# Attention with a filler: a step of two key blocks and four heads in place of four key blocks and two heads

## The chip, the cores and the metric

The kernel runs on one core of a Trainium2 chip. A core has engines with queues of their own: TensorE (PE in the profile; its weight loads are PEld), VectorE (DVE), ScalarE (ACT), GpSimd (POOL) and SyncE (SP), which here issues most of the transfers. The metric is device microseconds of one execution. The times before the change are 1333.11, 1337.48 and 1337.88 us; the median is 1337.48 us.

## The reference

The input x has 2048 tokens of 640 features. Two branches start from the same layer norm, and are added to x:

```python
xn = layernorm(x)
q, k, v = split(xn @ wqkv)              # 32 heads of 20 features
p = softmax(q @ k.T * 20 ** -0.5)       # 2048 x 2048 for each head
A = concat_heads(p @ v) @ wo
y = layernorm(xn)
B = gelu(y @ w1 + b1) @ w2 + b2         # 640 -> 1536 -> 640
out = x + A + B
```

## The kernel before, in words

**Precision.** All products are made of 16-bit or 32-bit parts so that the sum is nearly fp32. Queries and keys are stored as a high and a low fp16 half; a stack of three times 20 rows (high with high, high with low, low with high) and one row for a shift gives 61 rows, so that two heads lie in rows 0 to 60 and 64 to 124 of one tile. The exponentials `p` are fp32. Key blocks (128 keys each, 16 in all) are of two kinds, by `SPLIT = (1, 1, 0, 0) * 4`. In a split block V lies as two fp16 halves, and p is used as its upper 16 bits (read in place as bf16) and a lower half `low`, an fp16 tile that VectorE makes with one subtraction (`rest`, line 762). In an unsplit block p and V are multiplied as fp32, and each such product shows as two rows of the profile.

**Stages.** A first stage (to about 225 us) normalizes x, projects queries, keys and values, and splits the weights. Then the attention runs, and between its instructions the MLP (branch B) and, at the end, the output projection are laid as a filler. What is left of the projection follows the last attention step.

**The attention before.** The loops run over pairs of heads and halves of the queries (`ORDER`, 32 visits), over two chunks of 512 queries (`cc`), and over groups of `GRP = 4` key blocks. For each key block `scores` issues two matmuls (two heads, at the same time in two row halves of TensorE) into a tile of two PSUM banks (pool `psS`, three tiles), and one exponential of 128 x 1024 on ScalarE (line 750). `pv` multiplies a finished group with V (line 779). Its result tile `o` has 128 rows in four quarters of 32; each quarter takes products of its own, and four products for four quarters run at the same time in four column strips of TensorE. Before, the quarters 2a and 2a+1 hold two partial sums of head a, which are added much later. After 16 key blocks ScalarE copies `o` to `ev` (line 800), and `unload` writes the parts and the sums of the exponentials to `opart` and `lpart` in DRAM. For every 4 to 6 heads, `finish` reads them back, adds the two parts, divides by the sums, splits the result into fp16 halves and writes it to `oscr`, from where the projection takes it.

**What sets the order.** The program is written under a manual schedule: each engine executes in the order in which Python emits. A step emits: scores of two key blocks; `tick()`, which advances the side work (the gelu of the MLP on VectorE and ScalarE, the finishes, the loads of the next stack, each a generator that does one piece a tick; `patient` generators wait where other side work took time); the lower half of the first block; `other()`, which emits a chunk of the filler by a running credit (`rate = 1.265`); scores of the other two key blocks; `tick()`; the lower halves still open; and `pv` of the group before. The gelu of a pair of hidden blocks (lines 966 to 981) starts when its last filler matmul has been emitted, and takes five ticks: it reads the PSUM tile `pu` (966), adds the bias and squares (968, 970), forms the tanh's argument (972), waits for the tanh on ScalarE (977), and then makes and splits the result (979 to 981). SP issues the loads of the next stack (`load_stack`, line 143), the stores of `ev` and the transfers of the finishes in one queue.

Of the kernel before, what the change touches and what calls it, by code (L numbers as in the profile page):

```python
# [33 lines left out]
GRP = 4  # L34
# [3 lines left out]
TAIL = 12  # L38
ORDER = ([(g, hf) for g in range(TAIL) for hf in range(2)] + [(g, hf) for hf in range(2) for g in range(TAIL, NPAIR)])
MC = 256  # L40
QKTOP = 512.0
EXPMASK = 0x7F800000


def mha_mlp_kernel(tc, x, wqkv, wo, w1, b1, w2, b2, out):
# [4 lines left out]
    with (  # L50
# [13 lines left out]
        opart = dram.tile([2, D, S], F32, name="opart")  # L64
        lpart = dram.tile([2, 2, H, S // 2], F32, name="lpart")
        linv = dram.tile([2, H, S // 2], F32, name="linv")
# [15 lines left out]
        ones = keep.tile([P, P], F32, name="ones")  # L82
# [60 lines left out]
        stacks = {}  # L143

        def load_stack(g, hf, ks=None):

            new = ks is None
            qs = stp.tile([P, S // 2], F16, tag="qs", name=f"qs{g}")
            if new:
                ks = stp.tile([P, S], F16, tag="ks", name=f"ks{g}")  # L150
            stacks[g, hf] = (qs, ks)
            cols = slice(hf * 1024, (hf + 1) * 1024)
            for a in range(2):
                b, r = 64 * a, (2 * g + a) * DH
                for i in range(3):
                    rows = slice(b + i * DH, b + (i + 1) * DH)
                    nc.sync.dma_start(qs[rows, :], qkscr[(0, 0, 1)[i], r : r + DH, cols])
                    if new:
                        nc.sync.dma_start(ks[rows, :], qkscr[(0, 1, 0)[i], D + r : D + r + DH, :])
                    yield  # L160
            for a in range(2):
                b = 64 * a
                nc.sync.dma_start(qs[b + 60 : b + 61, :], bscr[2 * g + a : 2 * g + a + 1, cols])
                if new:
                    nc.sync.dma_start(ks[b + 60 : b + 61, :], bscr[H : H + 1, :])
                yield

# [7 lines left out]
        with tc.tile_pool(name="pa", bufs=2) as pa, tc.tile_pool(name="pa1", bufs=1) as pa1, tc.manual_schedule():  # L175
            wv = pa1.tile([P, KD, 3, 2, D], F16, name="wv")

# [168 lines left out]
            def qk_out(c, tt, ps):  # L346
                hl = stp.tile([P, 2, 2, 512], F16, tag="ks", name="qkhl")
# [15 lines left out]
            def qk_sq(c, tt, hl):  # L363
                if tt % 2:
                    sq = stp.tile([P, S // 2], F16, tag="qs", name="sq").bitcast(BF16).rearrange("p (i t) -> p i t", i=2)
                else:
                    sq = pa.tile([P, 2, 512], BF16, tag="sq", name="sq", bufs=2)
                if c == 0:
                    nc.scalar.activation(sq, hl[:, 0], AF.Square)
                else:  # L370
                    nc.vector.tensor_mul(sq, hl[:, 0], hl[:, 0])
                pend.extend((c, 2 * tt + i, sq[:, i]) for i in range(2))
# [212 lines left out]
            for c in range(4):  # L585
# [48 lines left out]
                if c == 3:  # L634
                    stack = load_stack(0, 0)
# [32 lines left out]
        with ExitStack() as scope:  # L668
# [3 lines left out]
            ptp = pool(name="pt", bufs=2 * GRP - 1)  # L672
# [64 lines left out]
            nfin = 2 * len(UNITS)  # L737
# [4 lines left out]
            def scores(g, hf, cc, kb):  # L742

                qs, ks = stacks[g, hf]
                pt = ptp.tile([P, 2, 512], F32, tag="p", name="p")
                ps = psS.tile([P, 2, 512], F32, tag="s", name="s")
                for a in range(2):
                    nc.tensor.matmul(ps[:, a, :], ks[64 * a : 64 * a + 61, kb * P : (kb + 1) * P],  # L748
                                     qs[64 * a : 64 * a + 61, cc * 512 : (cc + 1) * 512], start=True, stop=True)
                nc.scalar.activation(pt, ps, AF.Exp, scale=QS)  # L750
                return pt
# [5 lines left out]
            def rest(unit):  # L757

                kb, pt = unit[3:]
                if SPLIT[kb]:  # L760
                    low = ptp.tile([P, 2, 512], F16, tag="low", name="low", bufs=GRP)
# [3 lines left out]
            evs = {}  # L765

            def pv(units):

                g, hf, cc, kb0 = units[0][:4]
                if kb0 == 0:
                    pv.o = psO.tile([P, 512], F32, tag="o", name="o")
                    pv.begun = set()
                last = units[-1][3] == NKB - 1

                def product(q, src, v0, t):
                    nc.tensor.matmul(pv.o[32 * q : 32 * q + 32, :], src[:, v0 - PAD * (1 - q % 2) :][:, :32], t,  # L779
                                     start=q not in pv.begun, stop=last, skip_group_check=True)  # L780
                    pv.begun.add(q)

                split = [(u[3], upper(u[4]), u[5]) for u in units if SPLIT[u[3]]]
                whole = [(u[3], u[4]) for u in units if not SPLIT[u[3]]]
                of16 = lambda kb, a: 2 * PAD + kb * 2 * VROW + (2 * g + a) * 2 * VW
                of32 = lambda kb, a: PAD + kb * VROW + (2 * g + a) * VW
                for kb, up, _ in split:
                    for a in range(2):
                        product(2 * a, vhalf, of16(kb, a), up[:, a])
                        product(2 * a + 1, vhalf, of16(kb, a) + VW, up[:, a])  # L790
                for a in range(2):
                    for n, (kb, _, low) in enumerate(split):
                        product(2 * a + n % 2, vhalf, of16(kb, a), low[:, a])
                for a in range(2):
                    for n, (kb, pt) in enumerate(whole):
                        product(2 * a + n % 2, vfull, of32(kb, a), pt[:, a])
                if last:
                    if cc == 0:
                        evs[g, hf] = m1.tile([P, 2, 512], F32, tag="ev", name="ev")
                    nc.scalar.activation(evs[g, hf][:, cc], pv.o, AF.Copy)  # L800
                    if cc == 1:
                        unload(g, hf, evs.pop((g, hf)))

            def dma(g, hf):

                return (nc.scalar if (g, hf) == ORDER[-1] else nc.sync).dma_start

            def unload(g, hf, ev):
                cols = slice(hf * 1024, (hf + 1) * 1024)
                direct.extend([ev] if (g, hf) == ORDER[-1] else [])  # L810
                for p in range(0 if direct else 2):
                    dma(g, hf)(lpart[p, hf, 2 * g : 2 * g + 2, :].rearrange("a (c t) -> a c t", c=2),
                                      ev[PAD + DH + VW * p :: 64])
                    for a in range(2):
                        q0, r = 64 * a + PAD + VW * p, (2 * g + a) * DH
                        dma(g, hf)(opart[p, r : r + DH, cols].rearrange("d (c t) -> d c t", c=2),
                                          ev[q0 : q0 + DH])
                if g + 1 in ENDS:
                    fins.append(finish(g + 1 - UNITS[ENDS.index(g + 1)], g + 1, hf))
                    if len(fins) == 1:  # L820
                        patient.append(finishing())
                        runner[:] = patient[-1:]
# [520 lines left out]
```

## Time and profile before

| | before |
|---|---|
| median of three runs | 1337.48 us |
| span of the profiled execution | 1337.9 us |
| PE busy | 1325.8 us (99%) |
| ACT busy | 1128.0 us (84%) |
| DVE busy | 1055.1 us (79%) |
| exponentials (L750) | 1024 of 1050 ns |
| lower halves (L762) | 512 of 1218 ns |
| evacuations (L800) | 64 of 618 ns |
| DMA moved | 129.54 MB |

The span of the profiled execution agrees with the largest of the three runs, 1337.88 us. A group of instructions reads: line, engine, operation, out<-in, shapes, count | busy time, mean ns of one | idle time of the engine before them, and what ended it. In the timeline, each row has its start, its length, and how many instructions were merged. A matmul's length holds its latency, so throughput is read from the distance of starts. In the table by windows, the columns are the window, its length, and the busy time with the count of instructions of PE, PEld, DVE, ACT and POOL, then the granted clock of TensorE, the share of the DMA engines, and GB/s.

### The profile page before, as it was taken

The page shows a single profiled execution, that of the slowest core. Times are in us where ns is not written, and L with a number is a line of the kernel's source. Part 1 is how long each engine was busy: PE and PEld are TensorE (multiplying, and loading weights), DVE is VectorE, ACT ScalarE, POOL GpSimd, SP SyncE. Part 2 cuts the span into 40 slices and gives each one's busy share as a digit, 9 for nine tenths or more (in the row PEclk, how much of TensorE's full clock was granted, in tenths as well). Part 3 has the DMA queues.
Part 4 walks back from the last instruction along what each step waited for, and adds up shares of the span by engine and source line. Part 5 has one row for each costly group of instructions (what it writes and reads, how often), then busy time and mean ns, then how long its engine had stood idle before and what let it go on. Part 6 is the DMA issues. An engine that isn't in the chain of part 4 may idle for free.

```text
span 1337.9 us, 29042 instructions
## 1 busy us (share of the span) xinstructions
PE 1325.8 (99%) x11635; PEld 586.7 (44%) x11635; DVE 1055.1 (79%) x1431; ACT 1128.0 (84%) x1306; POOL 37.5 (3%) x86
## 2 busy tenths in 40 slices
PE   9999899999999999999999999999999999999998
PEld 6645456444434343434343443344443434333366
DVE  7656754998788989878897879888879888997742
ACT  7844334999999999999999999999999999999900
POOL 3010000000000000000000000000000000000000
PEclk9999899999999999999999999999999999999999
DMA  9778723021203232212322132223032323334375
GB/s 279 254 196 176 136 79 104 15 59 39 66 28 103 61 83 81 63 48 59 111 63 81 33 93 66 75 69 94 19 80 71 93 66 87 118 95 118 105 218 188
DMA packets 100326, 129.54 MB, mean 97 GB/s; under 512 B 24292, under 2 KB 66664, under 8 KB 100188
## 3 DMA queue, kind: packets, MB, share of 16 engines
q1 hardware_dynamic: 96652, 120.25, 31.6%
q0 software_dynamic: 2912, 6.90, 2.8%
q8 instruction: 92, 1.51, 0.5%
q10 hardware_dynamic: 624, 0.51, 0.1%
q14 instruction: 46, 0.38, 0.1%
HBM read 82.14 MB, written 42.51 MB: 93 GB/s over the span
## 4 chain that ended last, share of the span: by engine, by line
PE 87%; DVE 6%; DMA 4%; ACT 1%; issue 1%; SPq 0%; ACTq 0%; DVEq 0%
PE o L779 30%; PE s L748 20%; PE py L1061 13%; PE pu L1031 11%; PE z L1146 5%; PE qkp L337 5%; PE vp L410 3%; DVE low L762 2%; DMA xt<-in_A_x_dram 1%; DMA xnt<-row 1%; DMA qkscr<-qkhl 1%; DVE st L255 1%; DVE qkhl L353 1%; ACT p L750 1%; DMA wos<-in_A_wo_dram 0%
## 5 line engine op out<-in xcount | busy, mean ns | idle before, releaser
L750 ACT ACTIVATE p<-s 128x1024 f32<-128x1024 f32 x1024 | 973.9, 1050 | 33.1 <-PE s L748 27.1
L762 DVE TENSOR_TENSOR low<-p 128x1024 f16<-128x1024 f32 x512 | 614.3, 1218 | 144.8 <-ACT p L750 144.0
L779 PE MATMUL o<-p,vfull 128*32 128x512 bf16 (+1 forms) x4096 | 429.0, 493 | 0.0
L748 PE MATMUL s<-qs,ks 61*128 61x512 f16 x2048 | 311.4, 381 | 0.2 <-ACT p L750 0.2
L748 PEld LDWEIGHTS <-ks 61*128 61x128 f16 x2048 | 61.2, 94 | 278.4 <-issue 276.1
L1061 PE MATMUL py<-w2t,hT 128*128 128x320 f16 x1152 | 178.5, 300 | 0.0
L1031 PE MATMUL pu<-xm,w1t 128*128 128x256 f16 x1440 | 178.2, 273 | 0.1
L1031 PEld LDWEIGHTS <-w1t 128*128 128x128 f16 x1440 | 131.0, 98 | 64.0 <-issue 50.2
L1061 PEld LDWEIGHTS <-hT 128*128 128x128 f16 x1152 | 102.3, 98 | 88.1 <-issue 53.9
L337 PE MATMUL qkp<-xnt,wv 128*128 128x512 f16 x600 | 131.1, 379 | 1.3 <-issue 1.3
L779 PEld LDWEIGHTS <-vfull 128*32 128x32 f16 x3072 | 59.9, 95 | 138.4 <-issue 106.9
L779 PE MATMUL o<-low,vfull 128*32 128x512 f16 x1024 | 101.3, 377 | 0.1
L337 PEld LDWEIGHTS <-wv 128*128 128x128 f16 x600 | 58.2, 98 | 71.0 <-issue 1.6
L779 PEld LDWEIGHTS o<-p,vfull 128*32 128x32 f32 x2048 | 61.7, 108 | 53.2
L410 PE MATMUL vp<-wv,xnt 128*128 128x320 f16 x480 | 69.5, 306 | 3.7 <-DVE qkhl L353 3.7
L1146 PE MATMUL z<-w1t,ot 128*128 128x320 f16 x480 | 67.4, 299 | 0.0
L352 ACT ACTIVATE qkhl<-qkp,qks 128x1024 f16<-128x1024 f32 (+1 forms) x24 | 23.1, 964 | 46.3 <-PE qkp L337 26.6
L410 PEld LDWEIGHTS <-xnt 128*128 128x128 f16 x480 | 47.9, 100 | 23.8 <-issue 3.7
L1146 PEld LDWEIGHTS <-ot 128*128 128x128 f16 x480 | 46.0, 98 | 22.9 <-issue 5.5
L353 DVE SCALAR_TENSOR_TENSOR qkhl<-qkp,qks,qkhl 128x1024 f16<-128x1024 f32 (+1 forms) x24 | 26.5, 1104 | 32.9 <-ACT qkhl L352 32.9
L1103 DVE SCALAR_TENSOR_TENSOR acc<-z,sc,acc 128x320 f32<-128x320 f32 x32 | 17.5, 549 | 37.3 <-PE z L1146 37.2
L800 ACT ACTIVATE ev<-o 128x512 f32<-128x512 f32 x64 | 39.5, 618 | 2.2 <-PE o L779 2.1
(195 smaller groups left out, 670.4 us busy)
## 6 DMA issues: line engine op xcount, KB each, us to landing
qkscr<-qkhl SPq DMA_DIRECT2D x40, 256.0 KB
opart<-ev SPq DMA_DIRECT2D x124, 80.0 KB
ks<-qkscr SPq DMA_DIRECT2D x120, 80.0 KB
qs<-qkscr SPq DMA_DIRECT2D x192, 40.0 KB
oa<-opart SPq DMA_DIRECT2D x32, 240.0 KB
xt<-in_A_x_dram SPq DMA_DIRECT2D x16, 320.0 KB
xscr<-xnt SPq DMA_DIRECT2D x4, 1280.0 KB
xm<-xscr SPq DMA_DIRECT2D x8, 640.0 KB
```

The lines of the kernel that those rows point to most:

```text
L337: nc.tensor.matmul(ps[:, i, :], wv[:, k, q, a, mm * P : (mm + 1) * P], xnts[c][:, k, b, :], start=(k + n == 0), stop=(k == KD - 1 and n == 2))
L352: nc.scalar.activation(hl[:, 0, i0:i1], ps[:, i0:i1], AF.Copy, scale=a)
L353: nc.vector.scalar_tensor_tensor(hl[:, 1, i0:i1], ps[:, i0:i1], a, hl[:, 0, i0:i1], ALU.mult, ALU.subtract)
L410: nc.tensor.matmul(ps[:, hf, :320], xnts[c][:, k, a, j * P : (j + 1) * P], wv[:, k, 2, b, hf * 320 : (hf + 1) * 320], start=(n == 0), stop ...
L748: nc.tensor.matmul(ps[:, a, :], ks[64 * a : 64 * a + 61, kb * P : (kb + 1) * P], qs[64 * a : 64 * a + 61, cc * 512 : (cc + 1) * 512], star ...
L750: nc.scalar.activation(pt, ps, AF.Exp, scale=QS)
L762: nc.vector.tensor_sub(low, pt, upper(pt))
L779: nc.tensor.matmul(pv.o[32 * q : 32 * q + 32, :], src[:, v0 - PAD * (1 - q % 2) :][:, :32], t, start=q not in pv.begun, stop=last, skip_gr ...
L800: nc.scalar.activation(evs[g, hf][:, cc], pv.o, AF.Copy)
L1031: nc.tensor.matmul(ps[:, i], w1v[:, k, (f + i) // 4, a, fo_ : fo_ + P], xnt[:, k, b, :], start=(n == 0), stop=(n == 3 * KD - 1))
L1061: nc.tensor.matmul(ps[:, :320], hTs[mc][:, f, a, j * P : (j + 1) * P], w2v[:, f, b, hf * 320 : (hf + 1) * 320], start=(n == 0), stop=(n == ...
L1146: nc.tensor.matmul(ps[:, :320], ot[:, k, a, j * P : (j + 1) * P], wov[:, k, b, h * 320 : (h + 1) * 320], start=(n == 0), stop=(n == 3 * KD ...
```

## The change

A step is now `GRP = 2` key blocks for four heads. The visits run over eight sets of four heads (`q`); the first six visits take all four chunks of 512 queries, and the last two sets are visited twice, for two chunks each (`VISITS`). For a key block, `scores` is called for two pairs of heads, and the two exponentials of 128 x 1024 fill the halves of one tile of 128 x 2048. With `SPLIT` as it was, steps alternate: one has two split blocks, the next two unsplit ones. `pv` gives each of the four heads one quarter of `o`, which takes all its products, so no parts are added later, and `o` is copied out once for four heads (32 times). `rest` makes the lower half of four heads with one instruction of 128 x 2048; that of the second block of a step is emitted in the step after it. The pool of p holds four tiles of 2048 for seven of 1024, that of `low` two for four.

Queries and keys are loaded apart: queries for each chunk of 512, keys in two halves of 1024. A half of the keys is emitted in a few ticks after the first step of a visit (second half), or after the fifth step of the last chunk before (first half). The finishes work on 512 queries of one chunk, 24 of them for 12, and have no addition. The tile `ones` moves to a pool of the first stage. The projection of a piece of 256 tokens may start when its chunk of 512 is finished.

```diff
-GRP = 4
+GRP = 2
+VISITS = ([(q, tuple(range(NCC))) for q in range(LATE)]
+          + [(q, ccs) for ccs in ((0, 1), (2, 3)) for q in range(LATE, NQ)])
...
+        def load_keys(v, half):
+            q = VISITS[v][0]
+            ks = stp.tile([P, 2, S // 2], F16, tag="ks", name="ks")
+            kss[v, half] = ks
+            cols = slice(half * 1024, (half + 1) * 1024)
+            for a in range(2):
+                for i in range(3):
+                    nc.sync.dma_start(ks[64 * a + i * DH : 64 * a + (i + 1) * DH], rows_of(qkscr[(0, 1, 0)[i]], D, q, a, cols))
+                    if i != 1:
+                        yield
...
-            ptp = pool(name="pt", bufs=2 * GRP - 1)
+            ptp = pool(name="pt", bufs=2 * GRP)
...
+            def scores(v, cc, kb, pair, pt):
+                qs, ks = qss[v, cc], kss[v, kb // 8]
                 ps = psS.tile([P, 2, 512], F32, tag="s", name="s")
                 for a in range(2):
+                    rows = slice(64 * a, 64 * a + 61)
+                    nc.tensor.matmul(ps[:, a, :], ks[rows, pair, kb % 8 * P : (kb % 8 + 1) * P], qs[rows, pair, :],
+                                     start=True, stop=True)
+                nc.scalar.activation(pt[:, 2 * pair : 2 * pair + 2], ps, AF.Exp, scale=QS)
...
-                    low = ptp.tile([P, 2, 512], F16, tag="low", name="low", bufs=GRP)
+                    low = ptp.tile([P, 4, 512], F16, tag="low", name="low", bufs=2)
                     nc.vector.tensor_sub(low, pt, upper(pt))
...
+                def products(src, at, t):
+                    for h in range(4):
+                        nc.tensor.matmul(pv.o[32 * h : 32 * h + 32, :], src[:, at(h) : at(h) + 32], t[:, h],
+                                         start=not pv.begun, stop=last, skip_group_check=True)
+                    pv.begun = True
+                split = [u for u in units if SPLIT[u[2]]]
+                for u in split:
+                    for s in range(2):
+                        products(vhalf, of16(u[2], s), upper(u[3]))
+                for u in split:
+                    products(vhalf, of16(u[2], 0), u[4])
+                for u in units:
+                    if not SPLIT[u[2]]:
+                        products(vfull, lambda h: PAD + u[2] * VROW + (4 * q + h) * VW, u[3])
...
-                    nc.vector.tensor_add(o0, o0, o1)
...
                     for kb in range(kb0, kb0 + GRP):
-                        units.append([g, hf, cc, kb, scores(g, hf, cc, kb)])
-                        if kb % 2 == 0:
-                            continue
+                        pt = ptp.tile([P, 4, 512], F32, tag="p", name="p")
+                        units.append([v, cc, kb, pt])
+                        for pair in range(2):
+                            scores(v, cc, kb, pair, pt)
                         tick()
-                        if kb % GRP == 1:
-                            rest(units[0])
+                        if kb % GRP == 0:
+                            if prev and SPLIT[prev[1][2]]:
+                                rest(prev[1])
                             credit += rate
                             other()
                         else:
-                            for u in units[1:]:
-                                rest(u)
+                            if SPLIT[kb - 1]:
+                                rest(units[0])
                             if prev:
                                 pv(prev)
```

335 lines of the change are left out of this document (138 added, 197 removed).

## The prediction

> **What bounds the kernel now.** I read the busy times and the chain first, then a stretch of the attention phase, then the groups, then the timelines of one step.
>
> ```profile
> span 1337.9 us, 29042 instructions
> ...
> PE 1325.8 (99%) x11635; PEld 586.7 (44%) x11635; DVE 1055.1 (79%) x1431; ACT 1128.0 (84%) x1306; POOL 37.5 (3%) x86
> ...
> PE 87%; DVE 6%; DMA 4%; ACT 1%; issue 1%; SPq 0%; ACTq 0%; DVEq 0%
> ```
> ```profile
> 300.00:1200.00 900.00, 899.83 (x8439) 360.94 (x8441) 767.06 (x915) 870.87 (x975) 12.73 (x15) 1.00 0.26 72
> ```
> ```profile
> L750 ACT ACTIVATE p<-s 128x1024 f32<-128x1024 f32 x1024 | 973.9, 1050 | 33.1 <-PE s L748 27.1 <-ACT p L750 0.4
> L762 DVE TENSOR_TENSOR low<-p 128x1024 f16<-128x1024 f32 x512 | 614.3, 1218 | 144.8 <-ACT p L750 144.0
> ...
> L800 ACT ACTIVATE ev<-o 128x512 f32<-128x512 f32 x64 | 39.5, 618 | 2.2 <-PE o L779 2.1
> ...
> L966 DVE TENSOR_TENSOR u<-pu,r2f 128x512 f32<-128x512 f32 x48 | 32.8, 683 | 0.2
> L977 ACT ACTIVATE w<-w 128x512 f32<-128x512 f32 x48 | 32.0, 666 | 0.0
> ```
>
> In the 900 us from 300 to 1200 TensorE is busy 899.83 us at a granted clock of 1.00, ScalarE 870.87 and VectorE 767.06; the chain is 87% TensorE, and what ScalarE waits for before an exponential is TensorE's scores (27.1 of 33.1 us). A busy TensorE may hide waits, so I check one step (four exponentials) by start times:
>
> ```profile
> 704.17 0.60 PE L779 MATMUL o<-p,vfull 128*32 128x512 f32 x4
> 704.70 0.60 PE L748 MATMUL s<-qs,ks 61*128 61x512 f16 x4
> 705.24 1.81 PE L1031 MATMUL pu<-xm,w1t 128*128 128x256 f16 x15
> 706.98 0.61 PE L748 MATMUL s<-qs,ks 61*128 61x512 f16 x4
> 707.52 0.64 PE L779 MATMUL o<-p,vfull 128*32 128x512 bf16 x8
> 707.98 0.38 PE L779 MATMUL o<-low,vfull 128*32 128x512 f16 x4
> 708.20 1.03 PE L779 MATMUL o<-p,vfull 128*32 128x512 f32 x8
> 709.16 0.60 PE L748 MATMUL s<-qs,ks 61*128 61x512 f16 x4
> 709.70 1.81 PE L1031 MATMUL pu<-xm,w1t 128*128 128x256 f16 x15
> 711.44 0.39 PE L748 MATMUL s<-qs,ks 61*128 61x512 f16 x2
> ```
>
> Scores take 0.54, the filler 1.74, scores 0.54, then upper halves 0.46, lower halves 0.22 and unsplit blocks 0.96 (together 1.64): 4.46 us with no hole, and the next step repeats it. So TensorE's own work is the limit. A lighter ScalarE or VectorE gains nothing; either can only cost, by being late.
>
> **The change part by part.** *TensorE.* Per two steps the same products remain: 16 upper, 8 lower and 8 unsplit products of 512 columns (an unsplit one is two rows), only that the first 24 stand in one step and the unsplit ones in the next: 2 x 0.46 + 2 x 0.22 = 1.36, and 2 x 0.96 = 1.92; sum 3.28 = 2 x 1.64. Scores and filler keep counts and places. Gain 0. Bound below: the second half of the unsplit rows takes 0.53 (704.17 to 704.70), the first only 0.43 (0.96 - 0.53), so 0.10 us is paid on leaving. If only unsplit rows pay it, the change halves that: 128 x 0.10 = 13 us gained. I take 0, because 16-bit rows of the same 32-column form pay it too: 16 rows of 128 columns last 0.34 to the next start, while four turns at a quarter of 0.23 make 0.23:
>
> ```profile
> 200.92 0.41 PE L382 MATMUL norms<-sq,heads 128*32 128x128 bf16 x16
> 201.26 1.04 PE L337 MATMUL qkp<-xnt,wv 128*128 128x512 f16 x4
> ```
>
> *ScalarE.* The exponentials stay; 32 of 64 evacuations go, 32 x 0.618 = 20 us. *VectorE.* A row of 512 takes 683 ns, of 1024 1218, so 148 ns is fixed and 2048 take 148 + 4 x 535 = 2.29 us: 256 of them 586 us for 614; the finishes lose their additions. All of this lies beside TensorE: 0. [...]
>
> *The lower half comes later, in a larger piece.* This is the term that counts. Before, both lower halves of a group are issued in its own step and read a full step later. In the changed order, a split step issues that of its first key block beside its own second scores, and that of its second block only in the next step, after the first scores, while the products that read it are emitted behind that same step's second scores.
>
> Let t be the start of the second scores of a split step. Two exponentials end 2.4 us after their scores start (706.98 to 707.47 + 1.94; 709.16 to 709.59 + 1.94):
>
> ```profile
> 707.47 1.94 ACT L750 ACTIVATE p<-s 128x1024 f32<-128x1024 f32 x2 [0.20 <-PE s L748]
> 709.59 1.94 ACT L750 ACTIVATE p<-s 128x1024 f32<-128x1024 f32 x2 [0.17 <-PE s L748]
> ```
>
> The first block's scores lie 0.54 + 1.74 earlier, so its lower half can start at t + 0.1 and, at 2.29, end at t + 2.4; the second's can start at t + 2.4 and end at t + 4.7. TensorE asks for the second after 0.54 scores, 1.92 unsplit products of the step before, 0.54, 1.74, 0.54 and then the upper halves 0.92 and the first lower 0.22: t + 6.4. With nothing else on VectorE there is room of 1.7 us, and none is lost. But the activation of the filler stands in the same queue:
>
> ```profile
> 711.79 0.68 DVE L966 TENSOR_TENSOR u<-pu,r2f 128x512 f32<-128x512 f32 x1
> ...
> 713.84 1.22 DVE L762 TENSOR_TENSOR low<-p 128x1024 f16<-128x1024 f32 x1
> 714.98 0.68 DVE L972 SCALAR_TENSOR_TENSOR w<-w,u 128x512 f32<-128x512 f32 x1
> 715.58 1.21 DVE L762 TENSOR_TENSOR low<-p 128x1024 f16<-128x1024 f32 x1
> ...
> 718.45 0.68 DVE L979 SCALAR_TENSOR_TENSOR u<-w,u 128x512 f32<-128x512 f32 x1
> 719.17 0.49 DVE L980 TENSOR_SCALAR hT<-u,sc 128x512 f16<-128x512 f32 x1
> 719.69 0.75 DVE L981 SCALAR_TENSOR_TENSOR hT<-u,sc,hT 128x512 f16<-128x512 f32 x1
> ```
>
> L966 starts 0.35 after the last pu row (711.44 to 711.79), the group to L970 holds a lower half back by 2.05, L972 by 0.60, and the group L979 to L981 lasts 1.99. In the compiled order of the changed kernel 128 pairs of lower halves stand; between the two of a pair there is nothing 61 times, what was L972 24 times (with the group L966 to L970 ahead of the pair), the group L979 to L981 21 times, and one short row otherwise.
>
> Case A, 24 times: the activation begins at t + 0.35, the first lower half starts at t + 2.4, the second 2.2 + 0.6 later (2.2 since back-to-back rows overlap by 0.08: 713.84 + 1.22 against 714.98), it ends at t + 7.5: TensorE stands 1.1 us. Case B, 21 times: the tanh is queued behind the second exponentials, ends at t + 2.4 + 0.67, then 1.99, then 2.2: t + 7.3, 0.9 us. Where the filler chunk is 9 rows and not 15, TensorE asks 1.74 x 6/15 = 0.7 us sooner and both grow by that. Bounds: 24 x 1.1 + 21 x 0.9 = 45, and 24 x 1.8 + 21 x 1.6 = 77 us. I take 50, near the lower end: with a short chunk TensorE's step (0.54 + 1.04 + 0.54 + 1.64 = 3.76) is under four exponentials (973.9/1024 x 4 = 3.80), so there it has waits on ScalarE to give. Below the lower end: if start-up and hand-over are 0.4 us shorter per event than read here, 45 x 0.7 = 32. Behind a late lower half only TensorE waits; scores, filler and exponentials all shift with it, so it adds to the end.
>
> [...]
>
> *Keys and queries.* Keys come in halves, each emitted over the 3 steps before its use, where whole stacks came 8 groups ahead. SP needs, at 0.33 each, 16 loads, 5 stores and 2 loads of a finish in the 3 x 4.46 = 13.4 us:
>
> ```profile
> L159 SPq DMA_DIRECT2D ks<-qkscr x120: 281/329/1500, 211.4 to 1225.0; - x120
> ```
>
> That is 7.6 us, and 5.8 are left for waits of SP and for landing, which the page does not time for this queue. Bounds: 0, and half a step (2.2) at 9 visits, 20 us. I take 2, as the room is most of the need. Behind a late key half, all scores of the visit wait.
>
> *Ends.* The same 16 loads stand before the first scores, and 444 output rows after the last in both orders: 0. The last finish broadcasts over 512 columns and not 1024: half of these rows go,
>
> ```profile
> L931 PE MATMUL rb<-lt,sel 64*80 64x64 f32 x32 | 2.5, 234 | 0.0
> ```
>
> so 1.2 us less. The buffer pools (four tiles of 2048 for seven of 1024) give each tile back by a product that TensorE has issued before the next scores: 0.
>
> **Sum.** 1337.9 + 50 + 2 - 1 = 1389; the profiled span is 0.4 us above the median of 1337.48, which is as much as the runs differ otherwise, so I forecast 1388.
>
> **The rivals.** (1) *The cover holds.* VectorE idles 15% of the stretch (767 of 900), and if the compiled order lets it run ahead, the lower half is never last: 1337.5 - 1 + 2, about 1338. Against it: VectorE cannot start before the exponentials, and the room of 1.7 us is smaller than the 2.65 of case A whatever the mean load.
>
> (2) *The products get cheaper.* The 0.10 us on leaving belongs to the unsplit rows alone, and lateness is below the room: 1337.5 - 13 - 1 = 1323. It decides as soon as 13 us exceed the lateness, that is, below 0.3 us per case. For it: the 0.53 against 0.43. Against it: the 16-bit rows at 200.92, and the lateness has to be absent too.
>
> (3) *The key halves land late as well*: 1388 + 20 - 2, and with case A and B at their upper bound 1388 + 20 + 25 = 1433. For it: short notice. Against it: 5.8 us of room.
>
> **How the numbers follow.** A change of 0.5% (6.7 us) is about what this measurement can tell from none. Forecast (slower by lateness, own range 1365 to 1415): 0.74. Rival 1: 0.12, nearly all within 0.5%. Rival 2: 0.08, faster. Rival 3: 0.06, slower. So faster 0.08, same 0.11, slower 0.81. Forecast and rival 1 hold 0.86; the range from 1336 to 1414 takes in both but their edges.
>
> **What would show it.** Right: TensorE's rows that read `low` last longer than 0.38 in some 45 places, near the activation's rows, by about a microsecond; the chain names VectorE's lower halves and the activation for several per cent; `low` rows last 2.2 to 2.3 us x256, evacuations x32; the pair of unsplit and split product groups takes 3.28 together; ScalarE's idle time before exponentials grows, to TensorE. Wrong: those rows all near 0.38 (rival 1); product groups that sum to 3.18 (rival 2); TensorE's weight loads of scores waiting for a DMA of `ks` (rival 3).

## The result and the profile after

The changed kernel takes 1398.49 us (median of four runs, 1396.35 to 1401.37) against 1335.42 for the kernel before in the runs beside it (1333.11 to 1337.88): a ratio of 1.0479, 95% interval 1.0456 to 1.0502. It is 4.8% slower. The forecast was 1388, with 1336 to 1414 as its range. Of the edited kernels below, one execution (with nine blocks split) ran at a granted clock of 0.654 and took 1857.06 us; it is left out.

First the page of the changed kernel, its busy times and its chain of waits, and then the 900 us of the attention phase by engine (busy time and count of TensorE, its weight loads, VectorE, ScalarE and GpSimd, then granted clock, share of the DMA engines, GB/s):

```profile
span 1397.3 us, 28234 instructions
...
PE 1335.1 (96%) x11619; PEld 595.0 (43%) x11619; DVE 1036.5 (74%) x1191; ACT 1124.8 (80%) x1274; POOL 36.8 (3%) x85
...
PE 60%; DVE 23%; ACT 6%; DMA 5%; issue 4%; SPq 1%; DVEq 0%; ACTq 0%; POOLq 0%
PE o L800 17%; DVE low L785 12%; PE s L772 12%; PE py L1016 8%; PE pu L986 8%; PE qkp L361 7%; ACT p L774 5%; PE z L1101 5%; PE vp L434 3%; DVE u L922 1%; DVE u L924 1%; DVE w L926 1%; DVE w L928 1%; DMA xnt<-row 1%; DVE u L935 1%
```
```profile
300.00:1200.00 900.00, 854.90 (x7929) 346.38 (x7928) 706.90 (x655) 815.44 (x892) 11.89 (x14) 1.00 0.21 56
```

TensorE, which before was busy 899.83 of these 900 us, now stands 45 of them, at the same granted clock of 1.00. The chain was 87% TensorE and 6% VectorE; now it is 60% and 23%, with the lower halves (L785) at 12% and the activation of the filler (L922 to L928 and L935) behind them. VectorE did not become the fuller engine: it is busy 707 us of the stretch, less than the 767 before. It is late, not full.

The groups by form (count, busy time, mean ns of one, idle time of the engine before them and its cause):

```profile
L774 ACT ACTIVATE p<-s 128x1024 f32<-128x1024 f32 x1024 | 974.2, 1032 | 100.4 <-PE s L772 97.1
L785 DVE TENSOR_TENSOR low<-p 128x2048 f16<-128x2048 f32 x256 | 580.5, 2286 | 125.1 <-ACT p L774 124.5
...
L800 PE MATMUL o<-low,vfull 128*32 128x512 f16 x1024 | 87.1, 379 | 52.0 <-DVE low L785 51.9
...
L816 ACT ACTIVATE ev<-o 128x512 f32<-128x512 f32 x32 | 19.2, 600 | 5.6 <-PE o L800 5.1
```

The change does what it says: 256 lower halves of 2048 columns at 2286 ns, 32 evacuations instead of 64. The third row is new: the products that read a lower half now stand 51.9 us for it, where in the kernel before these products stood 0.1 us in all (its row for L779, `o<-low,vfull`). The chain of waits by engine says how often (total us, times, the longest):

```profile
ACT p L774 <- PE s L772: 97.1, 168, 2.3
PE o L800 <- DVE low L785: 51.9, 46, 1.5
...
PEld L772 <- DMA ks<-bscr: 2.1, 3, 1.5
...
PEld L772 <- DMA ks<-qkscr: 1.4, 1, 1.4
```

Forty-six waits of 1.1 us on the mean. The timeline shows one of them, of the kind the prediction called case A. TensorE (start, length, rows merged):

```profile
444.59 0.60 PE L772 MATMUL s<-qs,ks 61*128 61x512 f16 x4
445.13 1.10 PE L800 MATMUL o<-p,vfull 128*32 128x512 bf16 x16
446.05 0.40 PE L800 MATMUL o<-low,vfull 128*32 128x512 f16 x4
447.78 0.40 PE L800 MATMUL o<-low,vfull 128*32 128x512 f16 x4 [1.33 <-DVE low L785]
448.11 0.60 PE L772 MATMUL s<-qs,ks 61*128 61x512 f16 x4
```

VectorE at that time:

```profile
440.57 0.69 DVE L922 TENSOR_TENSOR u<-pu,r2f 128x512 f32<-128x512 f32 x1 [0.53 <-PE pu L986]
441.30 0.69 DVE L924 TENSOR_TENSOR u<-u,b1t 128x512 f32<-128x512 f32 x1
442.02 0.69 DVE L926 TENSOR_TENSOR w<-u 128x512 f32<-128x512 f32 x1
442.63 2.28 DVE L785 TENSOR_TENSOR low<-p 128x2048 f16<-128x2048 f32 x1
444.83 0.69 DVE L928 SCALAR_TENSOR_TENSOR w<-w,u 128x512 f32<-128x512 f32 x1
445.44 2.29 DVE L785 TENSOR_TENSOR low<-p 128x2048 f16<-128x2048 f32 x1
```

The second lower half starts at 445.44, behind L928, though its exponentials had ended by 443.20 (the end of ScalarE's rows before those of the next step), and ends at 447.73; the product that reads it starts at 447.78. The two turns of lower products should be 0.22 apart and are 1.73. And case B, where the end of the activation stands between the two, TensorE first, then VectorE:

```profile
506.46 1.10 PE L800 MATMUL o<-p,vfull 128*32 128x512 bf16 x16
507.37 0.40 PE L800 MATMUL o<-low,vfull 128*32 128x512 f16 x4
508.42 0.40 PE L800 MATMUL o<-low,vfull 128*32 128x512 f16 x4 [0.65 <-DVE low L785]
```
```profile
501.37 2.29 DVE L785 TENSOR_TENSOR low<-p 128x2048 f16<-128x2048 f32 x1
504.17 0.69 DVE L935 SCALAR_TENSOR_TENSOR u<-w,u 128x512 f32<-128x512 f32 x1 [0.51 <-ACT w L933]
504.89 0.49 DVE L936 TENSOR_SCALAR hT<-u,sc 128x512 f16<-128x512 f32 x1
505.41 0.75 DVE L937 SCALAR_TENSOR_TENSOR hT<-u,sc,hT 128x512 f16<-128x512 f32 x1
506.08 2.28 DVE L785 TENSOR_TENSOR low<-p 128x2048 f16<-128x2048 f32 x1
```

A pair of groups where nothing is late shows what the products themselves cost now:

```profile
454.77 1.12 PE L800 MATMUL o<-p,vfull 128*32 128x512 bf16 x16
455.70 0.62 PE L800 MATMUL o<-low,vfull 128*32 128x512 f16 x8
456.25 0.61 PE L772 MATMUL s<-qs,ks 61*128 61x512 f16 x4
...
458.79 1.92 PE L800 MATMUL o<-p,vfull 128*32 128x512 f32 x16
460.65 0.60 PE L772 MATMUL s<-qs,ks 61*128 61x512 f16 x4
```

Split group 456.25 - 454.77 = 1.48, unsplit 460.65 - 458.79 = 1.86.

**Where the time went.** I cut both spans at the first and the last scores, and each stretch between into groups by start times, so that waits inside a merged row are counted too. "Excess" below is the length of a group of products, from its first start to the start of what follows, over the median of such groups.

| stretch, us | before | after | difference |
|---|---|---|---|
| to the first scores | 224.7 | 217.8 | -6.9 |
| first to last scores (attention) | 1045.5 | 1112.4 | +66.9 |
| last scores to the end | 67.7 | 67.1 | -0.6 |
| span | 1337.9 | 1397.3 | +59.4 |

The 66.9 us of the attention phase: excess of the split groups 63.3, where before's groups had 2.2, so +61.1; the two kinds of group at their medians, 1.857 + 1.469 = 3.326 against 2 x 1.644 = 3.288, 0.038 x 127 = +4.8; excess of scores 2.5 against 1.5, +1.0. Of the 63 us, 35.0 lie in the 24 places where L928 stands between the two lower halves (mean 1.46, 0.96 to 2.26), 23.6 in 19 places with the group L935 to L937 between (mean 1.24, 0.83 to 1.68), and some 5 in all other places. The -6.9 of the first stage is dealt with in the last experiment: it is not a gain of the change.

### The profile page after: what moved, and what is told of

Read it like the earlier page. It is cut to its first block, busy times and chain, and to the rows that moved or that the text cites. A ratio compares the mean times of both kernels' runs of the same rounds, so it can differ in the third digit from the quotient of the medians.

```text
span 1397.3 us, 28234 instructions
## 1 busy us (share of the span) xinstructions
PE 1335.1 (96%) x11619; PEld 595.0 (43%) x11619; DVE 1036.5 (74%) x1191; ACT 1124.8 (80%) x1274; POOL 36.8 (3%) x85
## 4 chain that ended last, share of the span: by engine, by line
PE 60%; DVE 23%; ACT 6%; DMA 5%; issue 4%; SPq 1%; DVEq 0%; ACTq 0%; POOLq 0%
PE o L800 17%; DVE low L785 12%; PE s L772 12%; PE py L1016 8%; PE pu L986 8%; PE qkp L361 7%; ACT p L774 5%; PE z L1101 5%; PE vp L434 3%; DVE u L922 1%; DVE u L924 1%; DVE w L926 1%; DVE w L928 1%; DMA xnt<-row 1%; DVE u L935 1%
## 5 line engine op out<-in xcount | busy, mean ns | idle before, releaser
L774 ACT ACTIVATE p<-s 128x1024 f32<-128x1024 f32 x1024 | 974.2, 1032 | 100.4 <-PE s L772 97.1
L785 DVE TENSOR_TENSOR low<-p 128x2048 f16<-128x2048 f32 x256 | 580.5, 2286 | 125.1 <-ACT p L774 124.5
L800 PE MATMUL o<-p,vfull 128*32 128x512 bf16 (+1 forms) x4096 | 386.5, 495 | 0.0
L800 PEld LDWEIGHTS <-vfull 128*32 128x32 f16 x3072 | 76.1, 95 | 181.2 <-issue 119.8
L800 PE MATMUL o<-low,vfull 128*32 128x512 f16 x1024 | 87.1, 379 | 52.0 <-DVE low L785 51.9
L800 PEld LDWEIGHTS o<-p,vfull 128*32 128x32 f32 x2048 | 53.3, 109 | 130.1 <-issue 130.1
L922 DVE TENSOR_TENSOR u<-pu,r2f 128x512 f32<-128x512 f32 x48 | 33.0, 688 | 50.6 <-PE pu L986 49.8
L434 PE MATMUL vp<-wv,xnt 128*128 128x320 f16 x480 | 66.9, 299 | 0.1
L953 DVE SCALAR_TENSOR_TENSOR xb<-py,sc,xb 128x320 f32<-128x320 f32 x32 | 17.5, 547 | 43.0 <-PE py L1016 43.0
```

The lines of the kernel that those rows point to most:

```text
L434: nc.tensor.matmul(ps[:, hf, :320], xnts[c][:, k, a, j * P : (j + 1) * P], wv[:, k, 2, b, hf * 320 : (hf + 1) * 320], start=(n == 0), stop ...
L774: nc.scalar.activation(pt[:, 2 * pair : 2 * pair + 2], ps, AF.Exp, scale=QS)
L785: nc.vector.tensor_sub(low, pt, upper(pt))
L800: nc.tensor.matmul(pv.o[32 * h : 32 * h + 32, :], src[:, at(h) : at(h) + 32], t[:, h], start=not pv.begun, stop=last, skip_group_check=True)
L922: nc.vector.tensor_mul(u, ps, r2f[:, None, :].to_broadcast([P, 2, MC]))
```

## The experiments

The theory: the second lower half of a split pair is late because of where it stands in VectorE's queue, behind the activation of the filler. Rivals: it is the coarse grain of 2048 columns; it is the pairing of the two split blocks in one step, whatever the queue; it is VectorE's mean load. "Beside it" is always the kernel before, in runs of the same time. Each diff is against the changed kernel, unless it says otherwise; line numbers shift by one or two where lines are added.

**Two subtractions for one.** The same place in the queue, a finer grain.

```diff
-                    nc.vector.tensor_sub(low, pt, upper(pt))
+                    for h in (0, 2):
+                        nc.vector.tensor_sub(low[:, h : h + 2], pt[:, h : h + 2], upper(pt)[:, h : h + 2])
```

> The lower half of four heads is made by two instructions of 128 x 1024, at the same place in VectorE's order; all else is the changed kernel. Theory (the second lower half is late because activation rows stand ahead of it in VectorE's queue): in the 24 places with the pu activation ahead, VectorE is busy from the activation on, so the end of the second lower half does not move; in the 19 with the tanh's rows between, neither; two instructions cost 0.1 us more per lower half. Time 1398 to 1408 us, waits of TensorE for lower halves 52 to 60 us. Rival (an instruction of 2.3 us is too coarse: it must wait for both exponentials, and gives nothing back before its end): it could start one exponential earlier, about 1 us less in each of 45 places, 1350 to 1360 us.

1400.83 us (one run; 1334.97 beside it). The groups and the waits of this run:

```profile
L786 DVE TENSOR_TENSOR low<-p 128x1024 f16<-128x1024 f32 x512 | 597.6, 1218 | 80.4 <-ACT p L774 80.0
...
L801 PE MATMUL o<-low,vfull 128*32 128x512 f16 x1024 | 102.0, 378 | 41.2 <-DVE low L786 41.0
```
```profile
PE o L801 <- DVE low L786: 41.0, 69, 0.7
```

Sixty-nine waits of 0.6 for 46 of 1.1, and an excess of the split groups of 66.1 us for 63.3: the lateness is handed over in two parts and is no smaller. The grain is not the cause. The one instruction of 2048 saves VectorE 17 us (580.5 for 597.6) which nobody waits for.

**The held-back lower half ahead of the activation.** `tick()` emits the finishes and the activation of the filler; here the lower half of the step before goes first.

```diff
+                        if kb % GRP == 0 and prev and SPLIT[prev[1][2]]:
+                            rest(prev[1])
                         tick()
                         if kb % GRP == 0:
-                            if prev and SPLIT[prev[1][2]]:
-                                rest(prev[1])
                             credit += rate
```

> The lower half of the second block is emitted before the tick of its step, so that no activation row stands between the two lower halves of a pair; all else is the changed kernel. Theory (place in the queue): the 19 places with the tanh's rows between (23.6 us) lose nothing any more, the 24 with the argument row between keep 1.46 - 0.6 = 0.86 us, as the activation's first rows are still ahead of the pair: 21 of 63 us are left, 1350 to 1362 us. Rival (size of the instruction or the mean load of VectorE): work and sizes are the same, so about 1398 us.

1372.77 us (one run): 26 us come back by moving two lines, but 11 more than the upper end of what I expected remain. The waits of this run:

```profile
PE o L800 <- DVE low L785: 18.3, 24, 1.7
...
PEld L772 <- DMA ks<-bscr: 6.0, 7, 2.8
PEld L772 <- DMA oscr<-oa: 4.4, 1, 4.4
```

The excess of the split groups falls from 63.3 to 32.9. Case B is gone. Some 24 us stay in 24 places, and there the timeline has the group L922 to L926 directly ahead of one of the two lower halves: that of the first key block is still emitted behind it, so this move undoes only half of the order. Another 8.8 us lie in four places of 0.6 to 4.5 without an activation near: the weight loads of scores wait 12.9 us for a DMA in all, where they waited 5.4 in the changed kernel; of the four places the profile names keys in two, queries in one and the store of a finish (`oscr`) in one. Behind the two longest of these waits of TensorE (2.5 and 4.2 us) the granted clock is 0.50 for 3.4 us each, which costs another 3 us in filler and scores (see the next experiment).

**One operation more on VectorE.** A reduction of 0.68 us ahead of the held-back lower half, 128 times; its result is not used.

```diff
+            idle = m1.tile([P, 1], F32, name="idle")
...
+                                nc.vector.tensor_reduce(idle, vfull[:, :512], AX.X, ALU.max)
                                 rest(prev[1])
```

> One more row of about 0.67 us (a maximum over 128 x 512 values that nothing reads) stands on VectorE before the second lower half of each of the 128 pairs; all else is the changed kernel. It adds 86 us of VectorE's work. Theory (a room of 1.0 to 1.7 us, used up where the activation stands): the 43 places that already wait grow by the whole row, 29 us, the 61 empty ones by about 0.1 (6 us), the 19 with one short row by about 0.4 (8 us): 1432 to 1448 us. Rival (mean load of VectorE, 74% of the span): the row fits into idle time, 1398 to 1405 us; rival (VectorE bounds every step): 1484 us.

1450.89 us (one run), 3 above the range. The reduction and the waits for lower halves in this run, group and wait:

```profile
L1166 DVE TENSOR_REDUCE idle<-vfull 128x1 f32<-128x512 f32 x128 | 86.8, 679 | 0.0
```
```profile
PE o L801 <- DVE low L786: 84.6, 62, 2.1
```

Of 86.8 us of added work, 52 reach the end, on an engine that idled 193 of 900 us. The excess of the split groups is 36 us larger: in the 24 places of case A it grows by 0.52 on the mean, in the 19 of case B by 0.64, nearly all of the 0.68 added. The 61 places with nothing else between the two lower halves absorb the added row (0.04 on the mean), and the 24 with another short piece of work there give 9 us; the 19 of them with one other row of 0.68 grow by 0.33 to 0.40 on the mean. So the room is more than one row of 512 and less than two.

Of the remaining 16 us, 12 lie in rows of filler and scores, and they are a matter of the clock. TensorE waits 1.9 us or more for a lower half 23 times in this run, and behind nine of these waits the granted clock is 0.50 for 3.4 us. One of them, TensorE and then the window:

```profile
561.81 0.40 PE L801 MATMUL o<-low,vfull 128*32 128x512 f16 x4 [1.94 <-DVE low L786]
...
562.92 2.85 PE L1017 MATMUL py<-w2t,hT 128*128 128x320 f16 x10
565.70 0.63 PE L773 MATMUL s<-qs,ks 61*128 61x512 f16 x4
```
```profile
562.40:565.80 3.40, 3.40 (x16) 1.44 (x14) 3.30 (x5) 1.94 (x2) 0.00 (x0) 0.50 0.59 176
```

From start to start the ten rows of filler take 2.78 us here; eight of them just before the wait take 1.19, from 556.84 to 558.03. Against the same rows of the changed kernel each such stretch costs 1.5 to 1.6 us, 14 in all (2 of them within the 36). In the changed kernel no wait for a lower half is longer than 1.5 us, and its first trace has no such stretch in the attention phase. Another 2 us are the first stage, which differs between executions (last experiment). Without the nine stretches the run would lie near 1437 us, inside the range (an estimate, 1450.89 less 14).

**Alternate blocks split.** Every step then has one split and one unsplit block, instead of two split ones in one step and none in the next. The queue's order stays.

```diff
-SPLIT = (1, 1, 0, 0) * (NKB // 4)
+SPLIT = (1, 0) * (NKB // 2)
```

> Split and unsplit key blocks alternate (8 of 16 are split as before), so that each step has one of each, and its lower half is made in its own step and read in the next; four heads, sizes and counts of all instructions are those of the changed kernel. Theory (the second block's lower half has too little room): one lower half a step has 3.0 us of room, nearly all waits of TensorE for lower halves go, product groups take 1.64 us again: 1328 to 1340 us. Rival (four heads a step, keys in halves, 2048-wide lower halves cost by themselves): 1370 us or more.

1346.64 us (median of five runs, 1345.23 to 1349.73), ratio 1.0084 (1.0054 to 1.0115): 52 of the 63 us come back with no operation added or removed. A group of products costs 1.645 again, as before the change. It ends 7 above the range. In its waits, the lower halves are nearly gone, and keys stand beside them:

```profile
PEld L772 <- DMA ks<-bscr: 4.5, 5, 2.4
PE o L800 <- DVE low L785: 4.1, 12, 0.5
```

The excess of the groups is 13.1 us, some 7 of it for lower halves and 5.7 in four places (1.25 to 1.54 each) where scores wait for a DMA: by the profile for keys in two of them (in one for queries as well), for queries alone in one, and for the store of a finish in one. Its first scores start at 223.2 in the profiled execution, which makes that span some 5 longer than one with an early start (see the last experiment).

**Keys a step earlier**, on top of alternate blocks.

```diff
-                        if v and cc == ccs[0]:
-                            sides.append(load_keys(v, 1))
-                    if kb0 == NKB // 2 and cc == ccs[-1] and v + 1 < len(VISITS):
-                        sides.append(load_keys(v + 1, 0))
+                    if cc == ccs[-1] and v + 1 < len(VISITS):
+                        if kb0 == NKB // 2 - GRP:
+                            sides.append(load_keys(v + 1, 0))
+                        if kb0 == NKB - GRP:
+                            sides.append(load_keys(v + 1, 1))
```

> The alternating version with one more edit: both key halves are emitted one step earlier (the first half after the fourth step of the last chunk before, the second after its eighth). Theory (the alternating version still loses about 6 us in four places where a key half lands late, and 8 us to late lower halves): 6 us less, 1339 to 1343 us, with no score row that waits for a key transfer. Rival (the places are waits of something else): unchanged, 1345 to 1350 us.

1337.82 us (one run), beside 1336.04, and 1 below the range. The excess of the groups falls from 13.1 to 7.7: the four late places are gone, and 11 waits for lower halves of 3.9 us in all remain. This is the gain of the edit; another 4 us of the difference between the two profiled spans are an earlier first stage (first scores at 219.0 for 223.2).

**And both lower halves ahead of `tick()`**, on top of the two edits above. Now each lower half goes ahead of the finishes and the activation that the same half step emits.

```diff
+                        if kb % GRP == 0:
+                            if prev and SPLIT[prev[1][2]]:
+                                rest(prev[1])
+                        elif SPLIT[kb - 1]:
+                            rest(units[0])
                         tick()
                         if kb % GRP == 0:
-                            if prev and SPLIT[prev[1][2]]:
-                                rest(prev[1])
                             credit += rate
                             other()
                         else:
-                            if SPLIT[kb - 1]:
-                                rest(units[0])
```

> As the last, and each lower half is emitted ahead of the tick of its place, so that no side work of the tick stands before it. Theory (place in VectorE's queue): the remaining 8 us of waits for lower halves go as well; only TensorE's own rows are left, 1330 to 1336 us, level with the kernel before although ScalarE has 20 us and VectorE 35 us less to do. Rival (lighter ScalarE and VectorE do shorten it once nothing is late): under 1325 us.

1330.92 us (median of ten runs, 1329.87 to 1334.68) against 1336.04 beside it (thirteen runs): 0.9961 (0.9943 to 0.9979), the fastest of all kernels here and a little faster than the one before. Its attention phase by engine, and its group of lower products:

```profile
300.00:1200.00 900.00, 899.88 (x8434) 360.39 (x8428) 752.08 (x715) 861.69 (x948) 11.93 (x14) 1.00 0.23 63
```
```profile
L800 PE MATMUL o<-low,vfull 128*32 128x512 f16 x1024 | 100.1, 377 | 0.1
```

TensorE is busy 899.88 of 900 us again, and nothing waits for a lower half. ScalarE has 9 us and VectorE 15 us less work in the stretch than in the kernel before, and the attention phase is 1043.9 us against 1045.5: of what the change takes from the two engines, almost nothing arrives. Part of the 5 us between the medians is the first stage (last experiment); against an execution of the kernel before whose first scores start as early, the span is 2.1 us shorter (1329.3 for 1331.4).

**The same order with the blocks in pairs.** The edits of the run above, but `SPLIT` left at (1, 1, 0, 0).

> The alternating version with both edits (keys a step earlier, lower halves ahead of the ticks), but with the pattern of split blocks of the changed kernel (two split, two unsplit). Theory (the room of the second block's lower half is too small even without other delays): between the lower halves of a pair only two activation rows stand now, in 24 places; the second ends at 0.35 + 0.7 + 2.2 + 1.4 + 2.2 = 6.9 us after the second scores' start, 0.5 to 1.2 us late: about 21 us, and 5 us for the product groups: 1350 to 1362 us. Rival (order and keys were all that was wrong, the pattern is neutral): 1329 to 1337 us.

1358.28 us (one run), 1334.11 beside it. The same work in the same order as 1330.92, 27 us slower by the pattern alone: 19 waits for lower halves (15.9 us by the rows, 21.6 as excess) and the dearer pair of groups (1.857 + 1.463). So order and pattern each are a cause: with both put right, nothing waits.

**More blocks split.** With TensorE the bound, an unsplit block costs it more than a split one: (1.857 - 1.469) / 2 = 0.19 us. I tried nine, then ten of sixteen on top of the fastest version, hoping to go below it.

```diff
-SPLIT = (1, 0) * (NKB // 2)                         # fastest version
+SPLIT = (1, 0) * 6 + (1, 1) + (1, 0)                # nine
+SPLIT = ((1, 0) * 2 + (1, 1) + (1, 0)) * 2          # ten
```

> As the last, with one more key block split (9 of 16, the fourteenth). Per four heads a split block costs TensorE 2 x 0.23 + 0.22 = 0.68 us, an unsplit one 0.96 or 0.93; VectorE gets 32 more lower halves of 2.29 us. Theory (TensorE bounds, the others have room): 32 x 0.27 = 9 us less than the last, 1321 to 1328 us. Rival (ScalarE's 1025 us and waits between the engines bound already): no change against the last; rival (the second block's lower half is late again): up to 32 us more, since it stands in the one place per chunk with short room.

> As the last, with 10 of 16 key blocks split (also the sixth and the fourteenth, the extra block of each half being the second of its step). Theory: another 9 us of TensorE's rows go, but ScalarE's own rows (974 + 19 + 31 us) then fill nearly all of the attention phase: 1314 to 1326 us. Rival (VectorE, with 64 more lower halves, becomes late): 1335 us or more.

Both became slower, nine with 1349.15 to 1351.04 us (three runs), ratio 1.0115 (1.0059 to 1.0172), ten with 1385.43, ratio 1.0378 (1.0329 to 1.0427). The waits for lower halves, of nine and then of ten:

```profile
PE o L800 <- DVE low L785: 14.5, 20, 1.8
```
```profile
PE o L800 <- DVE low L785: 41.1, 44, 2.7
```

A single step with two split blocks in eight, and 32 more lower halves on VectorE, bring the lateness back: over the medians of 1.469 and 1.645, 11.6 us lie in the 32 crowded groups of products and 8.5 in the 224 others (1.1 in the fastest version). No run parts the crowding from the added work here. With two such steps in eight VectorE is busy 822 of 900 us, and part of the 54 us over the fastest version is the clock: four waits of 1.9 to 2.7 us have a stretch at 0.50 behind them, some 6 us by the 1.5 to 1.6 that one cost above (an estimate).

**The first stage again.** In the table above, the changed kernel's first scores start 6.9 us earlier, though nothing in the prediction shortens that stage. I ran both kernels again, unedited.

> The kernel before, unedited, for a second trace of its first stage. Its first scores started at 224.7 us, those of the changed kernel at 217.8, and nine edited kernels lie between 217.1 and 223.2. Theory (the first stage differs from execution to execution): here the first scores start anywhere from 217 to 224.7. Rival (the changed program has a shorter first stage of its own): they start at 222 or later here too, and the attention phase of the changed kernel then costs some 67 us, of which its first stage gives 5 to 7 back.

> The kernel before once more, for a third trace of its first stage: by the theory of execution to execution anywhere from 217 to 224.7, by the rival of a shorter first stage in the changed program 222 or later.

> The changed kernel, unedited, once more: by the theory of execution to execution its first scores start anywhere from 217 to 224.7, by the rival at 220 or earlier. From the first to the last scores 1112 us as in its first trace, within 3, by both.

First scores at 218.0 and 225.5 us in the kernel before (224.7 in its first trace), at 218.5 in the changed kernel (217.8). The kernel before starts either way, so the early start is not the changed program's. Spans 1331.4, 1338.7 and 1398.3; attention 1045.7, 1045.5 and 1112.7, the same as in the first traces to 0.3. The waits of TensorE between 100 and 225 us tell the two kinds of execution apart; of the kernel before with the late start (first scores at 225.5), then with the early one (218.0):

```profile
PE vp L410 <- DVE qkhl L353: 3.5, 1, 3.5
```
```profile
PE vp L410 <- DVE qkhl L353: 0.4, 1, 0.4
```

Behind this wait the granted clock differs too. The stretch from 150 to 170 us of the same two traces:

```profile
150.00:170.00 20.00, 16.49 (x123) 10.27 (x121) 14.20 (x29) 9.06 (x13) 0.00 (x0) 0.91 0.78 160
```
```profile
150.00:170.00 20.00, 19.58 (x159) 13.35 (x158) 15.97 (x35) 10.25 (x16) 0.00 (x0) 1.00 0.72 184
```

In the first trace of the kernel before, with its wait of 3.7 us, it is 0.83 there. Start for start against the early execution, that trace loses 3.3 of its 6.7 us at the wait and 2.7 in the 6.8 us at half clock right behind it. The late one above loses 3.1 of its 7.5 us at the wait and 1.3 in 3.4 us at half clock behind it; another 2.0 are lost by 44 us, around a first stretch at half clock (from 10.8 us). Why VectorE's split of the projections (L353) is late in some executions is open. That the changed kernel was early in both traces, and edited ones in eight traces of nine, may be chance or a habit; too few traces tell. The cost of the change between executions of the same start is some 66 us, more than the 59 of the two first spans.

## Why the prediction was right, and where its sum was not

*What bounds the kernel* held. The fastest version shows it from the other side: with ScalarE and VectorE lighter and nothing late, TensorE is busy 899.88 of 900 us and the attention phase is as long as before to 1.6 us. "Gains nothing, can only cost by being late" is what the runs measured.

*The later lower half* held in mechanism and count: 24 places of case A and 21 of case B were forecast, and the trace has 46 waits, 24 of them with L928 between and 19 with the group from L935. The size did not hold. The step that failed is "I take 50, near the lower end", because steps with a short filler would have waits on ScalarE to give. Measured are 35.0 + 23.6 = 59 us in these places, 1.46 and 1.24 each: the middle of the ranges 1.1 to 1.8 and 0.9 to 1.6, and all of it reaches the end. TensorE had no such waits to give: in the whole kernel before, its scores stood 0.2 us for exponentials, and it was busy 899.83 of the 900 us from 300 to 1200, a row that the prediction itself shows. ScalarE did not absorb the lateness, its idle time grew by it, from 27.1 to 97.1 us for TensorE's scores, as scores stand behind the waiting product in TensorE's order.

*No gain from the products* was nearly right: 3.28 a pair was forecast, 3.326 measured against 3.288, a loss of 4.8 us and not the 13 us gain of rival 2. The cost of leaving is paid by the 16-bit rows too: a split group of 1.469 holds 1.36 of products and 0.11 more at its end. The changed kernel leaves as often as before, so there was nothing to halve. What the extra 0.04 a pair is, no run isolates; alternate blocks do not have it (1.645).

*The keys*: 2 us taken, 3.6 measured, in three places of 0.9 to 1.5 (at 639.7, 935.0 and 1075.5 us). They lie within the 63 us of the split groups, and the profile names keys in the first, queries in the second and both in the third. Rival 3 exists, at the low end of its bounds; the version with alternate blocks shows more (5.7 in four places), once most of the lateness of lower halves is gone.

*Ends*: nothing forecast but 1 us at the end; measured 0.6 at the end and a first stage whose length is the execution's. The base of the sum was an execution with the late start (1337.9), which hid 7 us: 1331 + 67 is the sum that the runs bear out. So it is in part luck that the forecast came as near as 10 us.

*Rival 1*, that the cover holds since VectorE idles 15%, fell, and the added reduction shows why in a number: of 86.8 us of work put on an engine with 193 idle us in 900, 36 came out as lateness at the products, and more behind them by the clock. The cover is not the mean idle time but the room of one place, the 1.7 us of the prediction (by the added reduction more than one row of 0.68 and less than two) less what else is queued there.

*The larger subtraction*: 2.29 us was estimated for 2048 columns from the rows of 512 and 1024, and 2286 ns was measured. Two instructions of 1218 for one of 2286 moved the time by 2 us in one run (1400.83 against a median of 1398.49, with runs from 1396.35 to 1401.37), which is no difference: the 17 us of busy time that the one instruction saves VectorE (580.5 for 597.6) were not on the path.

## What to carry to other kernels

Where one engine is full, as TensorE was here (899.83 of 900 us), a lighter second engine buys next to nothing (1.6 us of the attention phase in the fastest version), and a change of its order or grouping is costed place by place: when is the result asked for, when can the work start at the earliest, how long does it take, and what else of its own engine's queue stands in front? Work whose result is due soon goes ahead of work that is due later, and it is spread evenly over the steps; two due pieces in one step and none in the next cost 27 us here with the same work and the same order. Mean idle time says nothing of that: VectorE idled 193 of 900 us while its lower halves came late. And a wait can cost more than its length: behind nine of the 23 waits of 1.9 us or more with the added reduction, 3.4 us at a granted clock of 0.50 cost 1.5 to 1.6 us each, so look at the clock behind the longest waits.

## What the runs showed that I had not expected

- More split blocks are less work for TensorE (by the medians of the groups 0.19 us less for each) and made the kernel 20 and 54 us slower than the fastest version (nine and ten for eight): one crowded step in eight, with 32 more lower halves, was enough to bring lateness back.
- The pair of groups costs 3.326 when unsplit and split products stand in separate groups, and 3.29 when each group has both.
- The first stage takes 218 or 225 us in executions of the same program, at one wait of 3.5 us for VectorE that is 0.4 in the others, and at stretches of half clock behind it and before. That is a tenth of what the change costs, and a comparison of two spans alone puts it down to the change.
- Removing one wait uncovered the next: the weight loads of scores waited 5.4 us for a DMA in the changed kernel, and 12.9 with two lines moved; asking for the keys a step earlier took the late places away.
- Nine waits of TensorE of 1.9 to 2.1 us each had 3.4 us at half the granted clock behind them, for 14 us in all; fourteen others of at least 1.9 us in the same run had none, and what decides it no run here shows.
